# A new written order for a fused linear-attention and expert kernel: single products of zeros as units of the order, the first expert's w1 in two pieces, half of the last store on another queue

## The chip, the core and the metric

The kernel runs on one core of a Trainium2 chip. The core has five instruction streams that run beside each other: PE (TensorE, the matrix products; PEld are its weight loads), DVE (VectorE), ACT (ScalarE), POOL (GpSimd) and SP (SyncE, which here only issues DMAs). Each stream runs its instructions strictly in the order in which they were written, and waits on semaphores for the others. The metric is the device time of one execution in microseconds (us); lower is better.

## The reference

Linear attention over 8 batches, each of 8 heads, 576 positions and 64 features, followed by a mixture of 8 experts with a gate that may keep the expert of the position before:

```python
phi = lambda x: np.where(x > 0, x, np.exp(x) - 1.0) + 1.0
q_p, k_p = phi(q), phi(k)
kv  = einsum('bhsd,bhse->bhde', k_p, v);  z = k_p.sum(axis=2)
x   = einsum('bhsd,bhde->bhse', q_p, kv) / (einsum('bhsd,bhd->bhs', q_p, z)[..., None] + 1e-6)
x   = x.transpose(0, 2, 1, 3).reshape(B, S, 512)
logits = x @ w_gate                       # (B, S, 8)
local  = sigmoid(x @ w_local)             # below 0.5: take this position's own expert
for b in range(B):
    for s in range(S):
        fresh = argmax(logits[b, s])
        e = fresh if s == 0 or local[b, s] < 0.5 else prev
        prev = e
        out[b, s] = softmax(logits[b, s])[e] * (relu(x[b, s] @ w1[e]) @ w2[e])
```

## The kernel before

The kernel is written for the case that all positions of a batch keep the expert of its first position; a flag is computed on the way, and a general path behind it, which is not run here, handles everything else. So a batch needs one expert's weights, and they are known only when the logits of the batch's first position are there.

The work of one batch `b` is cut into named operations. Two of the eight heads lie in one 128-row tile, so a batch has two halves of four heads, numbered `n = 2b` and `n = 2b + 1`. For each half: loads `Lk`, `Lq`, `Lv` (SP); exponentials `E.k`, `E.q` (ACT), which give one part of phi; `E2` (the relu part) and `P` (the rest of phi); `VC` copies v next to a column of ones; `K` is the product k'v (PE, 64x64 tiles, f32), `KC` copies it out; `Q` transposes q (PE), `QC` copies it out; `N` is the numerator with the denominator in an extra column (PE, 64x64 tiles), `D` divides it (DVE) into x in bf16. `QL`, `QLC`, `NL`, `DL`, `XL`, `XLC` do the same for 64 of the 576 positions that are left over. Then, for the batch: `X` transposes x, `XC` copies it out; `R.b.0` computes the logits of the last chunk, which holds position 0, and `R.b.1` those of the other chunks, `RC` copies them out; `PK` picks the expert and looks it up in a small cache of three weight slots, `BK` keeps the cache's books; `W.b.0` and `W.b.1` (POOL) load w1 and w2 of the expert if it is not in the cache; `CW` copies them into the working tiles `w1cur` and `w2cur` (DVE); `S1`, `S2`, `S3` compute the gate's factor; `H.b.0` to `H.b.7` are x·w1 in eight chunks (PE, 128x128, bf16), `HC` their relu; `O0.b` and `O.b.0` to `O.b.4` are the product with w2, `OC` scales it out of PSUM into `yo` (or `yl` for the 64 left-over positions), `ST` stores it.

What runs when is written out by hand as one list of words, `ORDER` (lines 23 to 72). Every word is an operation; its instructions are added to the streams of their engines in the order of the list, and nothing is moved afterwards. A number behind a slash is the PSUM bank pair that the operation uses; an operation that uses a bank waits until the last user's result has been copied out. A `^` puts a copy on the other one of DVE and ACT than its default. Since each engine takes its own operations in the list's order, a word that stands earlier in the list also stands ahead of later ones on its engine, and whoever it waits for holds up what is behind it.

Three things in the list matter below. First, products of zeros: `fills` (line 111) is a table that puts so many `zero`·`zero` products of 128x512 on PE ahead of some operations; they compute nothing and keep PE at work while it would wait. Second, the first expert's weights: for batch 0 `weights` loads w1 straight into `w1cur`, in pieces whose columns are given by `FP` (line 224), and w2 into `w2cur`. `HOLD.0` and `HOLD.1` are two tiny DMAs on SP that read the last element of the first and of the second half of `w1cur`; they wait for that half to land, and so keep what is behind them on SP from being issued before. Third, the tiles `yo` and `yl` have two buffers each, so the result of batch b may be written only when the store of batch b - 2 has landed.

SP and ACT share eight completion semaphores for their DMAs, used in turn: a DMA that gets a semaphore waits until the last DMA on it has landed.

Of the kernel before, what the change touches and what calls it, by code (L numbers as in the profile page):

```python
# [23 lines left out]
Lq.0 Lk.1 FILL/0 Lv.1 Lv.1.1 Lv.0 Lk.0 Lq.1 Lv.0.1 E0.0 P0.0 E.k.1 CL.1 WT/1 E.q.0 P.k.1 QL.0/2 VC.1^  # L24
E2.q.0^ QLC.0 K.1/3 VC.1.1^ P.q.0.0 K.1.1 E.k.0 P.q.0 CL.0 Q.0/2 Lq.2 VC.0^ Lk.3 P.k.0 E.q.1 Lk.2 KC.1^
VC.0.1 QC.0 K.0/3 E2.q.1^ K.0.1 P.q.1.0 KC.0^ P.q.1 E.q.2 NL.0/2 N.0.0.1/3 DL.0 Lq.3 E.k.3 Lv.3 WG D.0.0.1
XL.0/2 Lv.2 Q.1/1 XLC.0^ R.0.0/2 QC.1 N.0.0.0/3 RC.0.0 D.0.0.0 W.0.0 E.k.2 N.0.1.1/2 N.0.1.0/1 PK.0 E2.k.3
D.0.1.1 E.q.3 D.0.1.0 BK.0 P.k.3 VC.3^ W.0.1 X.0.0/3 X.0.1/2 XC.0.0 XC.0.1^ K.3/1 E2.q.2^ E2.q.3^ R.0.1/3
HOLD.0 H.0.0/2 P.q.3 Lk.5 H.0.1/0 HC.0.0 P.q.2 H.0.2/2 HC.0.1 H.0.3/0 KC.3 RC.0.1 S1.0 QL.1/1 CW.0.0 Q.3/3
QLC.1 HC.0.2 H.0.4/1 E2.k.2 HC.0.3^ H.0.5/2 QC.3 P.k.2 Q.2/0 HC.0.4^ H.0.6/3 QC.2 VC.2 N.1.1.1/1 HC.0.5 Lv.5  # L30
K.2/0 Lq.4 S2.0 D.1.1.1 HC.0.6 Lv.4 Lk.4 N.1.1.0/2 KC.2 Lk.7 S3.0 NL.1/3 Lq.5 H.0.7/1 DL.1 O0.0/0 D.1.1.0
HC.0.7 E.k.5 XL.1/3 O.0.0 XLC.1^ N.1.0.1/1 E2.k.5^ OC.0.0 N.1.0.0/2 D.1.0.1 VC.5^ R.1.0/3 O.0.1/0 D.1.0.0
E.q.4 RC.1.0 PK.1 E2.q.4 X.1.0/1 O.0.2/2 OC.0.1 P.k.5 W.1.0 VC.4^ X.1.1/3 XC.1.0 O.0.3/0 Lv.7 XC.1.1^ P.q.4
E.k.4 R.1.1/1 Lq.6 K.5/3 OC.0.2 Lv.6 CW.1.0 E2.k.4 Lk.6 O.0.4/2 Lk.9 E.q.5 RC.1.1 P.k.4 H.1.0/1 KC.5^ OC.0.4
E2.q.5^ H.1.1/3 OC.0.3 P.q.5 HC.1.0 K.4/2 E.k.7 S1.1 Lq.7 H.1.2/0 E2.k.7 Lk.8 HC.1.1^ H.1.3/1 HC.1.2^ E.q.6
CW.0.1 QL.2/3 Q.4/0 QLC.2 HC.1.3 P.k.7 W.1.1 H.1.4/3 QC.4 H.1.5/1 E2.q.6^ HC.1.4 VC.7^ P.q.6 H.1.6/0 HC.1.5
Lv.10 K.7/3 KC.4 Lv.8 CW.1.1 HC.1.6 VC.6^ N.2.0.1/1 NL.2/2 KC.7 D.2.0.1 N.2.0.0/0 E.q.7 Lv.9 H.1.7/3 D.2.0.0
S2.1 Q.5/1 HC.1.7 E2.q.7^ E.k.6 O0.1/0 S3.1 QC.5 DL.2 O.1.0 O.1.1/3 P.q.7 OC.1.0 E2.k.6 BK.1 Lq.9 QL.3/2
E.k.8 XL.2/1 O.1.2/0 Lq.8 P.k.6 XLC.2^ QLC.3 E2.k.8^ OC.1.1 R.2.0/1 K.6/2 E.k.9 RC.2.0 PK.2 N.2.1.0/3 OC.1.2
Lk.10 N.2.1.1/1 KC.6 VC.8^ W.2.0 ST.0.0 D.2.1.0 NL.3/0 O.1.3/2 E.q.8 D.2.1.1 Lk.11 DL.3 W.2.1 Q.6/3 OC.1.3  # L40
P.k.8 XL.3/1 X.2.1/0 XLC.3^ X.2.0/2 QC.6 XC.2.1 O.1.4/1 CW.2.0 XC.2.0^ R.3.0/0 K.8/3 OC.1.4 E2.q.8^ E.q.9
N.3.0.1/2 RC.3.0 Lk.12 KC.8 P.q.8 R.2.1/1 ST.1.4 VC.9^ H.2.0/0 E2.q.9 VC.10 H.2.1/3 RC.2.1 D.3.0.1 Lv.13
HC.2.0 H.2.2/1 Lv.11 E2.k.9 Lq.10 BK.2 Q.7/0 ST.0.4 HC.2.1 P.k.9 H.2.3/2 QC.7 H.2.4/3 P.q.9 HC.2.2 HC.2.3
H.2.5/0 PK.3 E.k.10 Lq.11 H.2.6/1 HC.2.4^ W.3.0 K.9/2 S1.2 HC.2.5 CW.2.1 N.3.1.1/3 HC.2.6 Lk.13 N.3.1.0/0
S2.2 KC.9^ D.3.1.1 E.q.10 N.3.0.0/1 H.2.7/2 D.3.1.0 E.k.11 W.3.1 O0.2/3 HC.2.7^ E2.k.10 D.3.0.0 QL.4/0
X.3.1/2 QLC.4 S3.2 X.3.0/1 E2.k.11 O.2.0 Q.8/0 XC.3.1 E2.q.10 OC.2.0^ O.2.1/2 P.k.11 QC.8 XC.3.0 E.q.11
# [29 lines left out]
def kernel(  # L76
# [11 lines left out]
    nc = tc.nc  # L88
    P = 128
    B, H, S, Dh = q.shape  # L90
    D = H * Dh
    E = moe_w_gate.shape[1]
# [15 lines left out]
    NX = 3  # L108
    SLOTS = [2, 2, 2, 2]

    fills = {("WT",): 13, ("K", 1): 4, ("R", 0, 0): 5, ("X", 0, 0): 4, ("K", 3): 2}

    consts = ctx.enter_context(tc.tile_pool(name="consts", bufs=1))
    keep = ctx.enter_context(tc.tile_pool(name="keep", bufs=1))
# [876 lines left out]
```

## Time and profile before

| | us |
|---|---|
| three runs | 221.3, 221.81, 220.11; median 221.3 |
| the profiled execution: its own time | 219.5 |
| its span, first to last instruction | 217.7 |
| PE busy | 206.1 (95% of the span) |
| DVE busy | 177.8 (82%) |
| ACT busy | 131.3 (60%) |

All times inside the execution below are counted from the start of the span. The profiled execution took 219.5 us by the same clock as the runs, 1.8 us more than its span, and 1.8 us less than the median of the three runs. A row of the timeline gives start, duration, engine, line, operation, what is written and read, how many instructions were merged into the row, and in brackets the idle time ahead of it with what ended it. A row's duration ends with the last result, so the next row on the same engine may start up to 0.1 us earlier; where it matters, the time from one start to the next is used.

### The profile page before, as it was taken

The numbers are of one execution on the slowest core, as the hardware profiler recorded it, in microseconds if no ns is written. First come the engines' busy times: TensorE is split into PE (matmuls) and PEld (weight loads), VectorE is DVE, ScalarE is ACT, GpSimd is POOL, SyncE is SP. The second block draws the span as 40 slices with busy tenths as digits, with TensorE's granted clock in tenths as the row PEclk, the third lists the DMA queues.
The fourth block names the chain that finished last, engine by engine and source line by source line (L and its number), as shares of the span: only waits on it lengthen the run. The fifth ranks groups of instructions, "written<-read, shape, count | busy, mean of one in ns | idle before, by whom it ended". The sixth has DMA issues, their size and how long they took to land.

```text
span 217.7 us, 8573 instructions
## 1 busy us (share of the span) xinstructions
PE 206.1 (95%) x3704; PEld 150.5 (69%) x3719; DVE 177.8 (82%) x459; ACT 131.3 (60%) x197; POOL 13.6 (6%) x41
## 2 busy tenths in 40 slices
PE   7878799999999999999999999999999999999991
PEld 2466588657885798865889578875889578747640
DVE  0695988798999999998999989778897989586740
ACT  2687838699999999793358975483753302501110
POOL 4000500000200000300100000110000001100000
PEclk9889999999999999999999999999999999999999
DMA  5989999988975989999359878598320009999033
GB/s 190 369 248 380 215 183 237 334 318 306 360 266 175 308 322 285 343 210 203 66 189 307 311 274 287 104 181 145 123 99 3 5 15 370 177 162 268 5 132 121
DMA packets 24447, 46.77 MB, mean 215 GB/s; under 512 B 2124, under 2 KB 9808, under 8 KB 23508
## 3 DMA queue, kind: packets, MB, share of 16 engines
q1 hardware_dynamic: 16324, 37.49, 49.5%
q0 software_dynamic: 7392, 8.41, 24.7%
q8 instruction: 31, 0.51, 0.9%
q10 hardware_dynamic: 688, 0.26, 0.5%
q14 instruction: 12, 0.10, 0.1%
HBM read 61.88 MB, written 9.44 MB: 328 GB/s over the span
## 4 chain that ended last, share of the span: by engine, by line
PE 77%; DMA 11%; ACT 4%; DVE 3%; issue 2%; POOLq 0%; ACTq 0%; DVEq 0%
PE hps L556 26%; PE yps L578 22%; PE kvps L306 7%; PE nps L357 6%; DMA w1s<-in_moe_w_dram 5%; PE tq L317 5%; PE yps L582 3%; DMA kraw<-in_k_dram 3%; DMA kraw<-in_moe_w_gate_dram 3%; PE tx L391 3%; PE lps L433 1%; PE npl L376 1%; DVE xb L345 1%; PE fill L744 1%; PE tql L330 1%
## 5 line engine op out<-in xcount | busy, mean ns | idle before, releaser
L556 PE MATMUL hps<-xT,w1cur 128*128 128x288 bf16 x512 | 67.0, 286 | 0.0
L578 PE MATMUL yps<-w2cur,hT 128*128 128x512 bf16 x243 | 58.4, 379 | 0.7
L556 PEld LDWEIGHTS <-w1cur 128*128 128x128 bf16 x512 | 48.7, 98 | 12.9 <-issue 0.6
L565 ACT ACTIVATE hT<-hps 128x576 bf16<-128x576 f32 x41 | 26.8, 660 | 36.4 <-PE hps L556 27.4
L578 PEld LDWEIGHTS <-hT 128*128 128x128 bf16 x256 | 24.0, 98 | 25.5 <-issue 0.3
L345 DVE TENSOR_TENSOR xb<-nps,rec 128x512 bf16<-128x512 f32 x32 | 22.1, 692 | 1.1
L281 DVE SCALAR_TENSOR_TENSOR fq<-fq,qraw 128x576 f32<-128x576 f32 (+1 forms) x32 | 22.4, 744 | 0.2
L306 PE MATMUL kvps<-vone,kraw 64*64 64x65 f32 x1152 | 21.1, 225 | 1.0 <-ACT kv L292 0.8
L306 PEld LDWEIGHTS kvps<-vone,kraw 64*64 64x64 f32 x1152 | 19.2, 140 | 3.5 <-ACT vone L292 1.7
L241 ACT ACTIVATE ek<-kraw 128x1152 f32<-128x1152 f32 x16 | 18.8, 1172 | 3.4 <-DMA kraw<-in_k_dram 3.4
L567 DVE TENSOR_SCALAR hT<-hps 128x576 bf16<-128x576 f32 x23 | 17.1, 753 | 4.2 <-PE hps L556 4.0
L274 DVE SCALAR_TENSOR_TENSOR kraw<-ek,kraw 128x1152 f32<-128x1152 f32 x14 | 18.9, 1349 | 0.7 <-ACT kraw L248 0.7
L241 ACT ACTIVATE fq<-qraw 128x1152 f32<-128x1152 f32 (+1 forms) x16 | 18.5, 1157 | 1.3 <-DMA qraw<-in_q_dram 1.3
L357 PE MATMUL nps<-kv,qT 64*64 64x65 f32 x1024 | 19.0, 219 | 0.2
L593 ACT ACTIVATE yo<-yps,pr 128x512 f32<-128x512 f32 x16 | 11.1, 691 | 11.4 <-PE yps L578 11.3
L357 PEld LDWEIGHTS nps<-kv,qT 64*64 64x64 f32 x1024 | 16.8, 134 | 1.5 <-issue 0.5
L317 PE MATMUL tq<-ident,fq 128*128 128x128 f32 x128 | 16.7, 274 | 0.0
L292 ACT COPY qT<-tq 128x512 f32<-128x512 f32 x28 | 15.9, 641 | 0.6 <-PE tq L317 0.6
L292 ACT COPY xT<-tx 128x1024 bf16<-128x1024 bf16 x9 | 9.1, 1014 | 9.9 <-PE tx L391 9.7
L317 PEld LDWEIGHTS tq<-ident,fq 128*128 128x128 f32 x128 | 14.4, 141 | 0.7
L595 DVE TENSOR_SCALAR yo<-yps,pr 128x512 f32<-128x512 f32 x16 | 11.7, 745 | 2.0 <-PE yps L578 1.9
L248 ACT ACTIVATE kraw<-kraw 128x1152 f32<-128x1152 f32 x10 | 11.7, 1170 | 0.0
(106 smaller groups left out, 222.2 us busy)
## 6 DMA issues: line engine op xcount, KB each, us to landing
kraw<-in_k_dram SPq DMA_DIRECT2D x16, 576.0 KB, 7.3
qraw<-in_q_dram SPq DMA_DIRECT2D x14, 576.0 KB, 5.3
vraw<-in_v_dram SPq DMA_DIRECT2D x14, 576.0 KB, 5.7
w1s<-in_moe_w_dram POOLq DMA_DIRECT2D x7, 1024.0 KB, 10.4
w2s<-in_moe_w_dram POOLq DMA_DIRECT2D x7, 1024.0 KB, 13.1
out_dram<-yo SPq DMA_DIRECT2D x14, 512.0 KB, 4.6
qraw<-in_q_dram SPq DMA_DIRECT2D x2, 512.0 KB, 4.0
w2cur<-in_moe_w_dram POOLq DMA_DIRECT2D x1, 1024.0 KB
```

The lines of the kernel that those rows point to most:

```text
L241: nc.scalar.activation(e[:, :, c0:c1, :], raw_, Act.Exp)
L274: nc.vector.scalar_tensor_tensor(r, e, 1.0, r, Alu.min, Alu.add)
L281: nc.vector.scalar_tensor_tensor(e[:, g], e[:, g], 1.0, r[:, g], Alu.min, Alu.add)
L292: (nc.scalar.copy if on_act(*name, act=act) else nc.vector.tensor_copy)(dst, src)
L306: nc.tensor.matmul(ps[g * PH:(g + 1) * PH, t, :W], lhsT=f[h, g, c, :], rhs=vo[h, g, c, :], start=(c == 0), stop=(c == C - 1))
L317: nc.tensor.transpose(ps[:, r, i * P:(i + 1) * P], ex_[n, "q"][:, 1 + i + (NC - 1) * r, :, :], identity=ident)
L345: nc.vector.tensor_tensor(dst, ps[:, :, :, :Dh].rearrange("p g (i t) e -> p g i t e", t=2), rec.rearrange("p g (i t o) -> p g i t o", t=2, ...
L357: nc.tensor.matmul(ps[o * PH:(o + 1) * PH, g, (il * 2 + t) * W:(il * 2 + t + 1) * W], lhsT=qT[n][g * PH:(g + 1) * PH, t, i * P + o * PH:i ...
L556: nc.tensor.matmul(ps[:, u, :HS], lhsT=w1b[:, kk, m * P:(m + 1) * P], rhs=xT[b][:, kk, u * HS:(u + 1) * HS], start=(kk == 0), stop=(kk == ...
L565: nc.scalar.activation(dst, src, Act.Relu)
L567: nc.vector.tensor_scalar(dst, src, 0.0, None, Alu.max)
L578: nc.tensor.matmul(ps, lhsT=hT[b][:, m, i * P:(i + 1) * P], rhs=w2b[:, m, :], start=(m == 0), stop=(m == FK - 1))
```

## The change

Four things change:

1. `ORDER` is another list of the same operations. Banks, the engine of many copies, and the places of loads and stores differ. Relus and scalings that DVE did are fewer: 16 of the 64 `HC` instead of 23, and 14 of the 40 `OC` instead of 20; ACT does the rest.
2. The products of zeros: the table `fills` keeps only 16 ahead of `WT` (the transposes of the gate weights), where it had 28 in five places. 24 single products, `Z.0` to `Z.23`, are operations of their own in the list, all of them ahead of `H.0.0`: six ahead of `WT`, the others between `K.1` and `X.0.0`. Three small 32x32 products of zeros stand at the very start.
3. `FP` has two pieces instead of three, so that w1 of batch 0 comes in halves (columns 0 to 511, 512 to 1023) instead of a quarter, a quarter and a half. `HOLD.1` moves from the middle of the list to just behind `HOLD.0`.
4. Of the last store (`ST.7.4`, the 64 left-over positions of batch 7) only the first half is issued by ACT; the second half goes to SP.

```diff
-Lq.0 Lk.1 FILL/0 Lv.1 Lv.1.1 Lv.0 Lk.0 Lq.1 Lv.0.1 E0.0 P0.0 E.k.1 CL.1 WT/1 E.q.0 P.k.1 QL.0/2 VC.1^
...
+Lq.0 Lk.1 Z.21 Z.18 Lv.1 Z.11 Z.0 Z.13 Lv.1.1 Z.14 Lk.0 Lv.0 Lq.1 Lv.0.1 E0.0 P0.0 E.k.1 CL.1 E.q.0 P.k.1
...
-    fills = {("WT",): 13, ("K", 1): 4, ("R", 0, 0): 5, ("X", 0, 0): 4, ("K", 3): 2}
+    fills = {("WT",): 16}
...
-        FP = (0, F // 4, F // 2, F)
+        FP = (0, F // 2, F)
...
-                    eng = nc.scalar if b == B - 1 else nc.sync
+                    eng = nc.scalar if b == B - 1 and h == 0 else nc.sync
...
+        for i in range(24):
+            op(("Z", i), lambda: work(1))
...
+            for _ in range(3):
+                nc.tensor.matmul(fill[:32, :32], lhsT=zero[:, :32], rhs=zero[:, :32], start=True, stop=True)
             for name in order:
                 work(fills.get(name, 0))
```

The list itself tells little; the streams that come of it do. Three places follow, each before and after. Line numbers in these rows are one higher after the change than before for the same operation. The names end in the buffer's number: `kraw_71` and `qraw_73` hold k and q of half 3, `vraw_74` its v, `qraw_72` and `kraw_70` are of half 2.

The first place is ACT from the copy of the second `K` on, before the change. In turn: `KC.0`, `E.q.2`, `E.k.3`, `XLC.0`, `QC.1`, `E.k.2`, `E2.k.3`, `E.q.3`, `VC.3`, `XC.0.1`:

```order
L292 COPY kv<-kvps 128x130
L241 ACTIVATE fq<-qraw_72 128x2x9x64
L241 ACTIVATE ek<-kraw_71 128x1152
L292 COPY xT<-txl 128x2x2x64
L292 COPY qT<-tq 128x2x256 x2
L241 ACTIVATE ek<-kraw_70 128x1152
L248 ACTIVATE kraw_71<-kraw_71 128x1152
L241 ACTIVATE fq<-qraw_73 128x2x9x64
L292 COPY vone_78<-vraw_74 128x18x64
L292 COPY xT<-tx 128x4x256
```

The same stretch of ACT after the change: `KC.0`, `E.k.3`, `QC.1`, `E.q.2`, `E2.k.3`, `E.q.3`, `VC.3`, `E2.q.3`, `XC.0.0`, `E.k.2`:

```order
L293 COPY kv<-kvps 128x130
L242 ACTIVATE ek<-kraw_71 128x1152
L293 COPY qT<-tq 128x2x256 x2
L242 ACTIVATE fq<-qraw_72 128x2x9x64
L249 ACTIVATE kraw_71<-kraw_71 128x1152
L242 ACTIVATE fq<-qraw_73 128x2x9x64
L293 COPY vone_78<-vraw_74 128x18x64
L249 ACTIVATE qraw_73<-qraw_73 128x1152
L293 COPY xT<-tx 128x4x256
L242 ACTIVATE ek<-kraw_70 128x1152
```

`XLC.0` has left for DVE and `E.k.2` stands behind the copy of x now; `E.q.2` has moved from ahead of `E.k.3` to behind `QC.1`, and `E2.q.3`, the relu of `qraw_73`, which DVE did, stands ahead of the copy of x.

The second place is SP around the holds, before:

```order
L139 DMA qraw_73<-in_q_dram 128x2x576
L139 DMA vraw_74<-in_v_dram 128x2x576
L139 DMA vraw_76<-in_v_dram 128x2x576
L510 DMA there<-w1cur 1x1
L139 DMA kraw_69<-in_k_dram 128x2x576
L139 DMA vraw_76<-in_v_dram 128x2x576
```

And after (`kraw_69` is `Lk.5`, k of the second half of batch 2):

```order
L140 DMA qraw_73<-in_q_dram 128x2x576
L140 DMA vraw_74<-in_v_dram 128x2x576
L140 DMA vraw_76<-in_v_dram 128x2x576
L511 DMA there<-w1cur 1x1 x2
L140 DMA kraw_69<-in_k_dram 128x2x576
L140 DMA vraw_76<-in_v_dram 128x2x576
```

`Lk.5` now waits for both halves of w1, where it waited for the first.

The third place is SP around the store of batch 1, `ST.1.0`, before (`yo_1363` is batch 1's result; the tiles' names carry their buffer's number here):

```order
L139 DMA qraw0_72<-in_q_dram 128x2x576
L139 DMA qraw1_73<-in_q_dram 128x2x576
L139 DMA vraw0_74<-in_v_dram 128x2x576
L139 DMA kraw3_71<-in_k_dram 128x2x576
L602 DMA out_0_dram<-yo_1363 64x2048 x2
L139 DMA qraw0_72<-in_q_dram 128x2x576
```

And after (`yo_1385` and `yl_1386` are batch 1's):

```order
L140 DMA qraw0_72<-in_q_dram 128x2x576
L140 DMA vraw2_76<-in_v_dram 128x2x576
L140 DMA vraw0_74<-in_v_dram 128x2x576
L140 DMA kraw3_71<-in_k_dram 128x2x576
L608 DMA out_0_dram<-yl_1386 64x256 x2
L603 DMA out_0_dram<-yo_1385 64x2048 x2
L140 DMA kraw1_69<-in_k_dram 128x2x576
```

The two stores of `yl` have come in ahead of the two stores of `yo`, which batch 3's first result (`OC.3.0`, the same buffer) has to wait for. `OC.3.0` was done by DVE and is done by ACT now, and PE's `O.3.2` takes the bank that `O.3.0` used, where it took another one before.

## What was predicted

> **What bounds the kernel.** I began with the page: the span, and the engines' shares of it.
>
> ```profile
> span 217.7 us, 8573 instructions
> ...
> PE 206.1 (95%) x3704; PEld 150.5 (69%) x3719; DVE 177.8 (82%) x459; ACT 131.3 (60%) x197; POOL 13.6 (6%) x41
> ```
>
> PE is busy nearly throughout. Next I cut the span where the first expert product starts (`H.0.0`, 27.47) and where the last product ends (212.87). A row of this view gives the stretch, its length, then busy time and instructions of PE, PEld, DVE, ACT and POOL, the granted clock, the DMA share and GB/s. The fourth row is a window inside the start.
>
> ```profile
> 0.00:27.47 27.47, 21.60 (x456) 14.37 (x458) 18.10 (x42) 18.64 (x26) 5.59 (x20) 0.94 0.93 279
> 27.47:212.87 185.40, 184.54 (x3255) 136.10 (x3264) 159.24 (x417) 112.70 (x171) 8.03 (x21) 1.00 0.74 208
> 212.87:217.70 4.83, 0.00 (x0) 0.00 (x0) 0.48 (x1) 0.00 (x0) 0.00 (x0) 0.93 0.33 106
> ...
> 8.50:12.50 4.00, 4.00 (x79) 2.66 (x80) 3.80 (x5) 3.70 (x8) 0.00 (x0) 0.57 1.01 362
> ```
>
> Three stages follow. In the middle one, 185.4 us, PE idles 0.9 us in all and the work is the same before and after, so a new order can win next to nothing there; it can only lose, by a new wait or by dearer neighbours. The start is 27.5 us in which PE is partly fed with zeros, because it waits for what DVE, ACT and the loads prepare: above all there can an order win. The end is 4.8 us of last stores.
>
> So I read how `H.0.0` is reached, on PE first (timeline; the row at 31.77 is from the chain of waits, where overlaps are cut off).
>
> ```profile
> 27.05 0.56 PE L433 MATMUL lps<-wg,xT 128*128 128x9 bf16 x16
> 27.47 4.08 PE L556 MATMUL hps<-xT,w1cur 128*128 128x288 bf16 x32
> 31.39 0.38 PE L330 MATMUL tql<-ident,fq 128*128 128x128 f32 x2
> 31.77 0.87 PE tq L317 x8
> 35.31 1.14 PE L556 MATMUL hps<-xT,w1cur 128*128 128x288 bf16 x8
> 36.38 0.70 PE L357 MATMUL nps<-kv,qT 64*64 64x65 f32 x32
> ```
>
> `R.0.1` (27.05) is followed at once by four `H`, at (31.39 - 27.47)/4 = 0.98 us each; `Q.3` (0.87) comes behind them. After the change `Q.3` stands ahead of `H.0.0`. The comparison is therefore fair if `H.0.0` after starts at 27.47 + 0.87 = 28.34: later is a loss, earlier a gain.
>
> **The start, term by term.** `R.0.1` needs both copies `XC.0.0` and `XC.0.1`. After the change the first of them is at the end of ACT's stretch that the order shows. These are ACT's rows before.
>
> ```profile
> 18.35 1.16 ACT L241 ACTIVATE ek<-kraw 128x1152 f32<-128x1152 f32 x1 [1.31 <-DMA kraw<-in_k_dram]
> 19.42 0.35 ACT L292 COPY xT<-txl 128x256 bf16<-128x256 bf16 x1
> 19.67 1.13 ACT L292 COPY qT<-tq 128x512 f32<-128x512 f32 x2
> 20.67 1.18 ACT L241 ACTIVATE ek<-kraw 128x1152 f32<-128x1152 f32 x1
> 21.73 1.17 ACT L248 ACTIVATE kraw<-kraw 128x1152 f32<-128x1152 f32 x1
> 22.79 1.17 ACT L241 ACTIVATE fq<-qraw 128x1152 f32<-128x1152 f32 x1
> 24.07 1.16 ACT L292 COPY vone<-vraw 128x1152 f32<-128x1152 f32 x1
> 25.26 1.01 ACT L292 COPY xT<-tx 128x1024 bf16<-128x1024 bf16 x1
> ```
>
> ACT stood idle until 18.35 for k of half 3 (`E.k.3`). Before, `E.q.2` was already done in that idle time; after, it stands behind it. From start to start: `E.k.3` 1.07 (18.35 to 19.42), `QC.1` 1.00, a full-size exponential 1.06, a relu 1.06. After the change ACT therefore runs: `E.k.3` 18.35, `QC.1` 19.42, `E.q.2` 20.42, `E2.k.3` 21.48, `E.q.3` 22.54, and `VC.3` could start at 23.60. It needs v of half 3, for which the two rows below (the issue on SP, and the landing of that load) give 16.86 + 7.1 = 23.96.
>
> ```profile
> 16.86 0.92 SPq L139 DMA_DIRECT2D vraw<-in_v_dram  x2
> ...
> DMA to landing us min/median/max: 7.1/7.1/7.1
> ```
>
> So `VC.3` at 24.0, `E2.q.3` at 25.1, `XC.0.0` at 26.2, done at 27.2; `R.0.1` 0.42, `Q.3` 0.87, and `H.0.0` at 28.5 to 28.6, against 28.34. I take +0.25 us. The lower end is the case that ACT does not end last (rival A, -0.8). For the upper end every operation counts with its full duration instead of start to start: 1.16, 1.13, 1.17 three times, 1.16, 1.17 and 1.01 from 18.35 on end at 27.5, and 0.56 and 0.87 behind them make 28.9: +0.6.
>
> The halves of w1 cost nothing in this sum. Rows of POOL's issue, the landing of the two quarters, the first hold on SP, the copy that waits for the second half, and the load behind the hold with its landing:
>
> ```profile
> 21.89 2.31 POOL L499 DMA_DIRECT2D w1cur<-in_moe_w_dram  x3 [18.13 <-DVE rec L344]
> DMA to landing us min/median/max: 5.0/5.4/5.7
> 28.41 0.75 SPq L510 DMA_DIRECT2D there<-w1cur  x1
> 29.20 0.37 SPq L139 DMA_DIRECT2D kraw<-in_k_dram  x1
> DMA to landing us min/median/max: 7.8/7.8/7.8
> 31.98 1.23 DVE L514 COPY w1s<-w1cur 128x4096 bf16<-128x4096 bf16 x1 [0.66 <-DMA w1cur<-in_moe_w_dram]
> ```
>
> The second quarter had landed by 28.41, so a first half that lands no later than that is there when `H.0.0` wants it at 28.5; at worst 0.1. POOL issues two pieces instead of three, some 0.77 sooner for w2 (2.31/3), which nobody waits for at that point. The zeros: 43 products instead of 28, all ahead of `H.0.0`, where PE waits anyway; cover is the idle time that the old ones filled, and if a row of them outlasts its wait, one costs about 0.22 (estimate from the `H` rows: 0.98/8 for 288 columns, so 0.22 for 512). The idle stretch ahead of `R.0.1` remains open for this, so zero.
>
> **The middle.** Two terms. First, PE's neighbours: eight products of `H` take 0.98 behind each other, but 35.31 to 36.38 = 1.07 where 64x64 products follow. Every such change of tile shape costs about 0.1. Counted in the two orders from `H.0.0` on, there are 50 such changes before and 52 after: +0.2, between 0 and 0.3. Over the whole list it is 60 against 71, since the zeros (128x128) stand between 64x64 groups.
>
> The Trainium skill, TensorEngine Tiling (Array Packing), section Key Properties, says that changing the tiling mode drains TensorE. The trace agrees, with 0.1 us each, and that rule speaks against this change: if all eleven added changes lay on the path, the term would be +1.1 instead of +0.2. Nine of them lie ahead of `H.0.0`, in PE's waiting time.
>
> Second, a new wait: `OC.3.0` needs the buffer that `ST.1.0` stores, and PE's `O.3.2` needs the bank that `OC.3.0` empties. Rows of that store before, with the landing of its first half; of a pair of `yl` stores; of PE at `O.3.1` and `O.3.2`; and ACT's group of such scalings (691 ns each):
>
> ```profile
> 113.50 1.14 SPq L602 DMA_DIRECT2D out_dram<-yo  x2
> DMA to landing us min/median/max: 7.6/7.6/7.6
> 120.07 1.98 SPq L607 DMA_DIRECT2D out_dram<-yl  x2
> 122.41 3.63 PE L578 MATMUL yps<-w2cur,hT 128*128 128x512 bf16 x16
> L593 ACT ACTIVATE yo<-yps,pr 128x512 f32<-128x512 f32 x16 | 11.1, 691 | 11.4 <-PE yps L578 11.3
> ```
>
> With two `yl` stores ahead (1.5 to 2.0 us of issue) the second `yo` store goes out at 115.6 to 116.1 rather than 114.1 and lands 7.6 us later, 123.2 to 123.7; as the second of the pair it may land up to 1.1 later (the pair's issue took 1.14): 123.2 to 124.8. `OC.3.0` takes 0.7, so the bank is free at 123.9 to 125.5. PE wants it at 122.41 + 3.63/2 + the moves above, about 124.6. The wait is 0 to 0.9; I take +0.35, the store's own row being the nearest and pointing to the lower half. The relus and scalings that go from DVE to ACT (13) cost nothing: ACT is 60% busy, and DVE, at 82%, is relieved.
>
> **The end.** Rows of SP's last two stores of `yo`, of ACT's two stores of `yl`, and SP's last long wait:
>
> ```profile
> 212.60 1.11 SPq L602 DMA_DIRECT2D out_dram<-yo  x2
> 213.40 1.68 ACTq L607 DMA_DIRECT2D out_dram<-yl  x2
> ...
> SPq L986 <- DMA out_dram<-yo: 2.1, 1, 2.1
> ```
>
> The second half of `yl` is issued at about 214.0 by ACT; SP is free at 213.7 and can issue it 0.3 earlier, but what SP's final wait ended on was a `yo` store. I take -0.15; between -0.45 (all of the gain and a shorter list on ACT) and +0.3 (the `yl` half queues behind `yo`).
>
> **Sum.** +0.25 + 0.35 + 0.2 - 0.15 = +0.65. The profiled execution would go from 219.5 to 220.15. The runs' median stands 1.8 above that execution; I carry the difference over: 221.3 + 0.65 = 222.0.
>
> **Rivals.** A: ACT is not what ends last. `XLC.0` no longer queues behind `E.k.3`; on DVE it can follow the division that the first row shows, at 18.5, and be done at 18.9 instead of 19.77. All of DVE moves up 0.87:
>
> ```profile
> 17.84 0.69 DVE L345 TENSOR_TENSOR xb<-nps,rec 128x512 bf16<-128x512 f32 x1
> 26.10 1.42 DVE L252 TENSOR_SCALAR qraw<-qraw 128x1152 f32<-128x1152 f32 x2
> 27.56 2.77 DVE L281 SCALAR_TENSOR_TENSOR fq<-fq,qraw 128x576 f32<-128x576 f32 x4
> ```
>
> Before, DVE had its copy of x done at 26.10, where the second row starts; now at 25.2. `P.q.3` (2.77/2 = 1.39, the third row holds it and `P.q.2`) ends at 26.6, `Q.3` at 27.5, and there `H.0.0` starts: 0.84 below 28.34, and 1.1 below my term, 220.9. For it: DVE is the bound of the start before. Against it: ACT's chain above, whose start at 18.35 is a load.
>
> B: the clock. In 8.5 to 12.5 us the granted clock was 0.57 with PE busy throughout. The profiled execution is 1.8 faster than the median, which could mean that other runs pay one more such window where it hurts, and that zeros prevent it. One window of 3.4 us at half clock costs at most 1.7: 222.0 - 1.7 = 220.3. The Trainium skill, TensorE: Matmul & The Clock Gate, section What's actually happening, has a free-running window of 3.4 us, by which the place of the half clock would differ from run to run; one trace cannot show that.
>
> C, on the other side: the second hold. `Lk.5` left at 29.20 behind the first; after, it leaves when the second half has landed, by the copy's row as late as 32.0, and lands 7.8 later, 39.8. ACT has `E.k.5` and `E2.k.5` (2.1) ahead of `HC.0.7` (0.7 at most), which `O.0.0` needs. Before, `O0.0` started at
>
> ```profile
> 40.02 1.67 PE L578 MATMUL yps<-w2cur,hT 128*128 128x512 bf16 x6
> ```
>
> so with its seven products `O.0.0` is due at 40.02 + 7 x 0.22 + 0.25 = 41.8. From a landing of 39.0 on PE waits: at 39.8 it is 0.8, and each us by which w1 lands later adds one; with 1 to 2 of them, since w2 shares its queue, 223.8 to 224.8. For it: 7.8 us for one load is the longest of these. Against: the expert is known up to 0.87 earlier, and SP's load has the queue to itself.
>
> D: nothing of this reaches the path: 221.3.
>
> **How the numbers follow.** The forecast 0.45, A 0.13, B 0.12, C 0.15, D 0.15. Within 1% of 221.3, which is about what a measurement of this kernel can tell from no change, means 219.1 to 223.5. Faster by more takes A and B together (219.2) and the end's gain: 0.16 with what I have overlooked. Slower: C's 0.15 and the upper ends of the forecast's terms (+0.6 + 0.9 + 0.3 + 0.3 = 2.1, 223.4): 0.18. The rest, 0.66, is the same. The range runs from A and B together to C's lower price: 219.2 to 224.0.
>
> **What would show it.** In the profile after: `E.k.3` idle ahead of it until about 18.4, then ACT without a gap to `XC.0.0` at 26 to 27, and `H.0.0` at 28.5; if `H.0.0` starts at 27.5, A is right. PE's waits would list `yps` on an ACT scaling near 125, of 0 to 0.9 us; a wait of `yps` near 42 on a relu is C. A granted clock of 1.00 in 8.5 to 12.5 shows that the zeros work; three runs close to the profiled one show B. PE's end should be 0.8 later than 212.87. A middle stage with PE idle over 2 us would prove the sum wrong.

## The result and the profile after

| | us |
|---|---|
| four runs after the change | 228.82, 226.1, 226.4, 227.39; median 226.9 |
| four runs before, on the same chip | 221.3, 221.81, 220.11, 220.09; median 220.7 |
| ratio after to before | 1.029, 95% interval 1.020 to 1.037 |
| the profiled execution after | 228.8 (span 227.2), the slowest of the four |
| the profiled execution before | 219.5 (span 217.7) |

The change makes the kernel slower by 5.7 to 6.2 us, depending on which of the runs before it is compared with. The forecast was 222.0 and its range ended at 224.0. Ratios here and below leave out disturbed executions, so they need not be the quotient of two medians; of the four runs of e4 and of e5 two remain each, and of the profiles of e4 and e11, which are disturbed, only the end of e4 is read.

First the page of the kernel after, its span and the engines' shares:

```profile
span 227.2 us, 8615 instructions
...
PE 212.2 (93%) x3734; PEld 152.3 (67%) x3734; DVE 170.0 (75%) x448; ACT 139.5 (61%) x208; POOL 13.3 (6%) x40
```

The span has grown by 9.5, PE's busy time by 6.1. About 2.9 of that are products of zeros (12.0 after, 9.1 before), all of it in the start, where they fill time in which PE waits; the half clock shown below adds 1.7. The stretches cut as in the prediction, at `H.0.0` and at PE's last product, then four short windows of the same view (length, then busy time and instructions of PE, PEld, DVE, ACT and POOL, granted clock, DMA share, GB/s):

```profile
0.00:30.49 30.49, 25.73 (x481) 17.12 (x481) 20.33 (x48) 19.22 (x26) 4.85 (x19) 0.94 0.94 273
30.49:220.58 190.09, 186.51 (x3256) 135.15 (x3253) 149.13 (x400) 120.31 (x182) 8.49 (x21) 0.99 0.69 199
220.58:227.19 6.61, 0.00 (x1) 0.00 (x0) 0.48 (x1) 0.00 (x0) 0.00 (x0) 0.67 0.33 108
127.34:130.26 2.92, 0.00 (x0) 0.00 (x0) 2.29 (x3) 0.74 (x2) 0.00 (x0) 1.00 1.00 323
130.26:134.50 4.24, 4.24 (x12) 1.56 (x12) 0.00 (x0) 3.63 (x5) 0.00 (x0) 0.60 0.74 302
11.00:14.60 3.60, 3.60 (x43) 2.88 (x44) 3.50 (x6) 2.98 (x5) 0.00 (x0) 0.53 0.78 241
```

All three stages lose. `H.0.0` starts at 30.49, which is 2.15 later than the fair reference of 28.34. The middle, 190.09, stands against 185.37 - 0.87 = 184.50 (`Q.3` has left it): 5.6 more. The end is 6.61 instead of 4.83: 1.8 more. Inside the middle PE does nothing for 2.92 us, and right behind that it works 4.24 us at a granted clock of 0.60. The clock's records have 0.5 from 130.61 to 134.02; that costs 3.41/2 = 1.7. Next, for whom PE waited (us in total, times, the longest):

```profile
PE yps L579 <- ACT yo L594: 2.9, 1, 2.9
PE nps L358 <- issue: 1.7, 2, 1.1
...
PE kvps L307 <- ACT vone L293: 0.9, 1, 0.9
PE tq L318 <- issue: 0.8, 1, 0.8
```

The first row is the new wait of the prediction, eight times its size. For the rows with "issue" the same view of before has only this one:

```profile
PE fill L744 <- issue: 0.2, 1, 0.2
```

After the change PE waits for nothing that the profile shows, in the middle of an operation, three times. These idle times are taken up below.

So the 9.5 us of the profiled execution go to: start 2.15, a third "issue" idle time at 44.90 0.61, the wait at 130 2.92, the half clock behind it 1.7, what is left of the middle 0.4 (5.6 less these three), the end 1.8. The sum is 9.6, for 9.5. The other three runs are 1.4 to 2.7 shorter than this one; two of them have a mean granted clock of 0.99 instead of 0.975. So the split holds for the profiled execution; how much each of these terms took in the other runs is not known.

**The store.** SP's rows around `ST.1.0`, then the pieces of the chain of waits (start, us, what) from its second store to PE:

```profile
115.11 0.37 SPq L140 DMA_DIRECT2D qraw<-in_q_dram  x1
115.53 1.76 SPq L140 DMA_DIRECT2D vraw<-in_v_dram  x2
117.34 0.47 SPq L140 DMA_DIRECT2D kraw<-in_k_dram  x1
117.85 1.96 SPq L608 DMA_DIRECT2D out_dram<-yl  x2
119.86 1.27 SPq L603 DMA_DIRECT2D out_dram<-yo  x2
```

```profile
120.51 8.91 DMA out_dram<-yo
...
129.52 0.70 ACT yo L594
130.22 0.04 issue
130.26 5.30 PE yps L579 x16
```

PE reached `O.3.2` at 127.34, which is the predicted 124.6 plus the 2.7 by which everything was late by then. The store was not: predicted were an issue at 115.6 to 116.1 and a landing 7.6 to 8.7 later; measured were 120.51 and 8.91.

**The end.** SP's rows behind PE's last products, and ACT's one:

```profile
218.11 1.24 SPq L608 DMA_DIRECT2D out_dram<-yl  x2
219.45 3.73 SPq L603 DMA_DIRECT2D out_dram<-yo  x4
221.14 0.58 ACTq L608 DMA_DIRECT2D out_dram<-yl  x1
223.28 0.54 SPq L608 DMA_DIRECT2D out_dram<-yl  x1
```

ACT is free at 221.72. SP, to which the second half was moved, comes to it only at 223.28, since the last of its four `yo` stores takes from 221.32 to 223.18.

**The idle times called "issue".** PE's rows at the first two of them:

```profile
22.05 0.50 PE L358 MATMUL nps<-kv,qT 64*64 64x65 f32 x17
23.63 0.46 PE L358 MATMUL nps<-kv,qT 64*64 64x65 f32 x15 [1.08 <-issue]
...
28.62 0.41 PE L318 MATMUL tq<-ident,fq 128*128 128x128 f32 x2
29.84 0.81 PE L318 MATMUL tq<-ident,fq 128*128 128x128 f32 x6 [0.81 <-issue]
```

One operation is cut in two. By the trace's count of PE's instructions (weight loads, products and a few of its sequencer) the three idle times begin behind the 705th, the 960th and the 1473rd: 255 and 513 apart. The page's list of DMA queues has one for instructions:

```profile
q8 instruction: 31, 0.51, 0.9%
```

These packets bring PE's own program: 29 of the 31 fall into PE's working time, one for every 259 of its 7512 recorded instructions (7512/29), and each has 16 KB (0.51 MB/31). In the trace the second, third and fifth of them land at 22.31, 28.40 and 43.47; PE goes on at 23.63, 29.84 and 44.90, 1.3 to 1.4 later each time. If a border lies at every 256th instruction, counted so that 705 is one, then 26 of the 28 packets of before that can be set against a border landed about 2 us or more before PE came to it, the other two 1.5 and 1.7; after, the three named ones landed 0.02, 0.36 and 0.60 before, and all others at least 1.5. In these two traces that separates the stalls from the borders without one.

The Trainium skill, Runtime: NRT & Kernel Launch, section Instruction fetch mechanics, has instructions streamed in 16 KiB blocks of 256, with the cost of a border mostly hidden. The block agrees with 255 and 513. That it is hidden holds for the trace before (0.16 us) and not for this one (2.5 us).

### The profile page after: what moved, and what is told of

It is laid out like the page before. It is cut to its first block, busy times and chain, and to the rows that moved or that the text cites. A ratio compares the mean times of both kernels' runs of the same rounds, so it can differ in the third digit from the quotient of the medians.

```text
span 227.2 us, 8615 instructions
## 1 busy us (share of the span) xinstructions
PE 212.2 (93%) x3734; PEld 152.3 (67%) x3734; DVE 170.0 (75%) x448; ACT 139.5 (61%) x208; POOL 13.3 (6%) x40
## 4 chain that ended last, share of the span: by engine, by line
PE 77%; DMA 11%; SPq 3%; ACT 3%; DVE 2%; issue 2%; ACTq 0%
PE hps L557 26%; PE yps L579 22%; PE kvps L307 8%; PE tq L318 6%; PE nps L358 6%; DMA out_dram<-yo 4%; DMA vraw<-in_v_dram 3%; PE yps L583 3%; DMA kraw<-in_k_dram 3%; PE tx L392 2%; PE lps L434 1%; SPq L140 1%; SPq L608 1%; ACT qraw L249 1%; DMA out_dram<-yl 1%
## 5 line engine op out<-in xcount | busy, mean ns | idle before, releaser
L579 PE MATMUL yps<-w2cur,hT 128*128 128x512 bf16 x256 | 60.7, 387 | 2.9 <-ACT yo L594 2.9
L557 PEld LDWEIGHTS <-w1cur 128*128 128x128 bf16 x512 | 48.9, 98 | 12.5 <-DVE pr L550 0.2
L566 ACT ACTIVATE hT<-hps 128x576 bf16<-128x576 f32 x48 | 30.8, 653 | 27.3 <-PE hps L557 27.3
L594 ACT ACTIVATE yo<-yps,pr 128x512 f32<-128x512 f32 x21 | 14.3, 689 | 20.8 <-PE yps L579 16.3
L318 PE MATMUL tq<-ident,fq 128*128 128x128 f32 x128 | 17.7, 284 | 0.9 <-issue 0.8
L596 DVE TENSOR_SCALAR yo<-yps,pr 128x512 f32<-128x512 f32 x11 | 8.2, 746 | 12.2 <-PE yps L579 12.2
L293 ACT COPY qT<-tq 128x512 f32<-128x512 f32 x26 | 14.8, 631 | 0.3
L568 DVE TENSOR_SCALAR hT<-hps 128x576 bf16<-128x576 f32 x16 | 11.9, 751 | 3.8 <-PE hps L557 3.8
L293 ACT COPY vone<-vraw 128x1152 f32<-128x1152 f32 (+2 forms) x13 | 13.6, 1049 | 0.5 <-DMA vraw<-in_v_dram 0.5
L747 PE MATMUL fill<-zero 128*128 128x512 bf16 x40 | 11.7, 427 | 0.0
```

What stands on the lines that cost most here:

```text
L293: (nc.scalar.copy if on_act(*name, act=act) else nc.vector.tensor_copy)(dst, src)
L318: nc.tensor.transpose(ps[:, r, i * P:(i + 1) * P], ex_[n, "q"][:, 1 + i + (NC - 1) * r, :, :], identity=ident)
L557: nc.tensor.matmul(ps[:, u, :HS], lhsT=w1b[:, kk, m * P:(m + 1) * P], rhs=xT[b][:, kk, u * HS:(u + 1) * HS], start=(kk == 0), stop=(kk == ...
L566: nc.scalar.activation(dst, src, Act.Relu)
L579: nc.tensor.matmul(ps, lhsT=hT[b][:, m, i * P:(i + 1) * P], rhs=w2b[:, m, :], start=(m == 0), stop=(m == FK - 1))
L594: nc.scalar.activation(dst, src, Act.Copy, scale=pr[:, i:i + 1])
```

## The experiments

Each kernel is compared with the kernel before, run on the same chip beside it (medians 221.1, 221.4 and 221.1 for the three groups of four). "Middle" is the time from `H.0.0` to PE's last product.

**e1: the store of batch 1 earlier.** In the list, `ST.1.0` goes ahead of `Lq.12`:

```diff
-E2.k.12^ Lq.12 H.3.5/0 ... D.4.0.0 ST.1.0 N.4.1.0/2
+E2.k.12^ ST.1.0 Lq.12 H.3.5/0 ... D.4.0.0 N.4.1.0/2
```

> The changed kernel with one word moved: ST.1.0, the two stores of yo of batch 1, stands ahead of the load of q (half 12) that SP holds back until 115.11 in the trace of after, instead of behind the two stores of yl. Theory 1 (the late store is the cause of PE's wait of 2.92 us at 130.26 and, through that idle time, of the half clock in the 3.4 us behind it): the store lands near 119, PE's yps wait is gone, the granted clock stays 1.00 around 130. Time about 226.9 - 2.9 = 224.0, and a profile that had the half-clock stretch gains 1.7 more. Rival (the time is only moved: the loads behind the store go out 1.2 us later and PE waits for one of them, or for the next store): 226 to 227, with a new wait of 2 us or more on PE between 120 and 145.

Measured: 225.5, ratio 1.020 (1.011 to 1.029), against 1.029. The stores went out at 111.74 and 112.28 and had landed by 120.74; PE's wait is gone, and the clock is full where it was halved. The window 115 to 135 of e1:

```profile
115.00:135.00 20.00, 19.52 (x426) 14.18 (x424) 16.11 (x47) 13.16 (x21) 0.55 (x3) 1.00 0.80 302
```

Of the 0.48 that PE lacks there, 0.38 is one "issue" idle time, in `K` at 120.31. The wait did not come back elsewhere, so theory 1 holds for the wait and for the clock. Profile against profile the middle is 3.8 shorter (186.32 against 190.09), and `H.0.0` comes at 30.96 instead of 30.49, with idle times of 0.81 and 1.63 called "issue" ahead of it. The median fell by 1.4 only, not by 2.9 or more. The profiled execution of after was its slowest; what its other runs paid for the wait is not on record, so this difference stays open.

**e2: `ST.1.0` and `ST.1.4` exchanged.**

```diff
-ST.1.4 H.3.7/0 HC.3.6 D.4.0.0 ST.1.0
+ST.1.0 H.3.7/0 HC.3.6 D.4.0.0 ST.1.4
```

> The changed kernel with ST.1.0 and ST.1.4 exchanged, so that the yo stores of batch 1 stand ahead of the yl stores as before the change; nothing else. Theory 1a (the issue of the two yl stores, 117.85 to 119.82 in the trace of after, is what makes the yo store late, as the prediction's term had it): the second yo store goes out 2.0 us sooner, at 118.5, lands at 127.4, OC.3.0 ends at 128.2, PE's wait is 0.9 instead of 2.9; time about 224.9. Rival (the landing is set by the queue of data, 8.9 us here against 7.6 before, and by SP's earlier wait until 115.11, not by those two issues): landing stays at 128.5 to 129.4, PE waits 2.0 to 2.9, time 226 to 227.

Measured: 226.25, ratio 1.025 (1.016 to 1.033). The second `yo` store went out at 117.17, 1.9 sooner than after (1.5 of the 3.3 is because everything was 1.5 earlier there). It took about 9.8 us to land instead of 8.9 (reckoned back from PE's start, 0.85 as in the chain of after), and PE still waited:

```profile
PE yps L579 <- ACT yo L594: 1.9, 1, 1.9
```

So half of the gain in issue was lost in landing: the two `yl` stores ahead are worth 1.0 of the 2.9, not 2.0. The rest is that the store stands behind four loads of 576 KB, of which the first waits for DVE; both theories had a part. The clock stayed at 1.00 behind this wait of 1.95.

**e3: the borders of the instruction packets moved.** 64 small products more and 8 large ones less, at the very start, where PE waits for the gate weights anyway:

```diff
-    fills = {("WT",): 16}
+    fills = {("WT",): 8}
...
-            for _ in range(3):
+            for _ in range(67):
```

> The changed kernel with 67 small 32x32 products of zeros at the very start instead of 3, and 8 instead of 16 products of 128x512 zeros ahead of WT: PE's stream grows by 112 instructions ahead of everything else, in time in which PE waits for the gate weights anyway (they land at 7.82). Theory 2 (PE's idle times that the profile calls issue, 1.08 at 23.63, 0.81 at 29.84, 0.61 at 44.90, are PE's own instructions arriving late: each ends 1.3 to 1.4 us after a 16 KB packet of the instruction queue has landed, at 22.31, 28.40 and 43.47; where such a packet falls in the stream is decided by the count of instructions ahead of it): the three idle times leave these products and turn up elsewhere or not at all; H.0.0 starts 0.8 to 1.9 us sooner than 30.49, time 224.5 to 226 if no new ones take their place. Rival (they come of the loads that fill the DMA queues at these times, wherever the packets fall): idle times of the same size at the same products, time 226 to 227.5.

Measured: 239.2, ratio 1.085 (1.075 to 1.096), 12 us slower than the changed kernel. The three idle times did move, but the new place is far worse than the old one. PE's waits in e3:

```profile
PE nps L358 <- issue: 5.4, 5, 1.5
PE yps L579 <- issue: 3.3, 2, 3.1
PE npl L377 <- ACT fq L242: 2.3, 1, 2.3
...
PE tq L318 <- issue: 1.2, 1, 1.2
```

What was expected of the time is missed by 13 us or more; that the place of the borders matters is what it shows, and e5 tells it from the number of products. 112 instructions further on, borders fall at both ends of runs of `N` and `K`: four of the times from border to border are about 2 us in this trace, where the shortest of after is 4.6. The row `npl` ends at a border too: the packet landed at 125.76, PE went on at 126.71, and the profile names ACT.

**e4: the last store as before the change.**

```diff
-                    eng = nc.scalar if b == B - 1 and h == 0 else nc.sync
+                    eng = nc.scalar if b == B - 1 else nc.sync
```

> The changed kernel with both halves of the last yl store on ACT, as before the change. Theory 3 (SP is the later queue: its last yo store is issued from 221.32 to 223.18 and the yl half goes out at 223.28, while ACT would be free at 221.72): the end after PE's last product shrinks from 6.6 to about 5.2 us, time about 225.5. Rival (the prediction's term: SP is no later than ACT, the half on SP gains 0.15): 226.9 to 227.1, with the end as long as before or longer.

Measured: 1.022 (1.012 to 1.032); that can't be told from after's 1.029 (225.05 and 226.72 in the two runs that remain). The end can: 5.55 us behind PE's last product, where after, e1 and e2 have 6.61, 6.53 and 6.55. The later kernels agree: 8.2 in e3 and 6.20 in e5, which store as after, and 5.3 to 5.8 in e8, e9, e10 and e12, which store as e4. SP is the later queue; theory 3 has the direction and about the size (it said 5.2).

**e5: the borders moved by one whole block.** 147 small products instead of 3 and no large ones ahead of `WT`, together 256 instructions.

```diff
-    fills = {("WT",): 16}
+    fills = {}
...
-            for _ in range(3):
+            for _ in range(147):
```

> The changed kernel with 147 small products of zeros at the very start instead of 3, and none of the 16 large ones ahead of WT: PE's stream grows by 256 instructions. The idle times called issue in the profile of after begin 255 and 513 instructions of PE apart, so a 16 KB packet is taken to hold 256 instructions, and with 256 more ahead every later packet border falls at the same product as after the change, while e3 with 112 more was 12 us slower. Theory 2 (the place of the borders decides): within 2 us of the changed kernel, 225 to 229, issue idle times only where after, e1 and e4 have them (first 50 us). Rival (the many small products, or the lost large ones, cost the 12 us, by the clock or by the length of the stream): 237 or more.

Measured: 226.77 and 229.02 in the two runs that remain, against 225 to 229 expected. From two runs that can't be told from the changed kernel (226.1 to 228.82); it is at least 8.5 less than the fastest run of e3, which has 80 small products fewer. PE's rows for "issue" are one, 0.8 us at 46.11, in the same `N` as in after. So it is the place of the borders that cost e3 its 12 us, not the number of small products. In the start of e5, unlike that of after, PE waited 3.4 for copies of v and worked at half clock from 29.07 to 32.49.

**e6: the kernel before, with its borders moved.**

```diff
-    fills = {("WT",): 13, ("K", 1): 4, ("R", 0, 0): 5, ("X", 0, 0): 4, ("K", 3): 2}
+    fills = {("WT",): 5, ("K", 1): 4, ("R", 0, 0): 5, ("X", 0, 0): 4, ("K", 3): 2}
...
+            for _ in range(64):
+                nc.tensor.matmul(fill[:32, :32], lhsT=zero[:, :32], rhs=zero[:, :32], start=True, stop=True)
```

> The kernel before with 64 small products of zeros at the very start and 5 instead of 13 large ones there: 112 instructions more ahead of everything, no other change. Theory 2: the kernel before is only fast with its own packet borders. Taking the times between borders from its trace, moved by 112 instructions, four intervals of 256 instructions would last 2.3 us or less, against 3.6 at the shortest as it is; summed over all intervals, what lacks to 4.2 us (about what a packet needs from one border until its instructions run, estimated from the three idle times of after) is 11.8 against 1.1. So 229 to 233, with issue idle times in N and K between 35 and 180 us. Rival (the new written order alone brings the idle times): 220 to 222.5.

Measured: 235.9, ratio 1.071 (1.063 to 1.079), 14.5 us above the kernel before with the same written order. PE's waits:

```profile
PE nps L357 <- issue: 3.5, 3, 1.6
PE yps L578 <- DVE xb L345: 2.2, 1, 2.2
PE lps L433 <- issue: 2.1, 1, 2.1
...
PE hps L556 <- issue: 1.7, 2, 1.4
```

More than the 229 to 233 expected: the idle times in the middle sum to 9.8, near the 11.8 reckoned, but two of them (2.11 at 127.5 and 2.24 at 161.8) were each followed by 3.4 us at half clock, which the reckoning left out. The second is the row put down to DVE; it counts among them since PE went on 1.54 after a packet had landed (160.26), with a border there.

**e7: the kernel before with w1 in halves.**

```diff
-        FP = (0, F // 4, F // 2, F)
+        FP = (0, F // 2, F)
```

> The kernel before with w1 of batch 0 in halves (FP in two pieces), HOLD.1 and all else as before. Theory 4 (a half is later than a quarter: in the trace of after the first half landed at 29.66, 7.7 us after its issue, in e2 PE waited 0.32 at 28.93 for it; the first quarter before had landed by 27.47): H.0.0 starts between 28.4 and 29.7 instead of 27.47 and waits for w1cur, H.0.1 and all behind follow; 1 to 2 us more, 222 to 223. Rival (the prediction's term, at most 0.1): H.0.0 by 27.6, 221 to 221.3.

Measured: 224.73, ratio 1.019 (1.014 to 1.024), 3.4 more. The first half landed 8.1 us after its issue, at 29.88, 1.5 later than both quarters together had been there before (28.39). PE's longest wait, and the window behind it:

```profile
PE hps L556 <- DMA w1cur<-in_moe_w_dram: 2.4, 1, 2.4
```

```profile
27.51:29.93 2.42, 0.01 (x2) 0.01 (x1) 2.42 (x4) 0.00 (x0) 0.00 (x0) 1.00 1.10 163
29.93:34.00 4.07, 4.07 (x20) 2.71 (x21) 2.25 (x7) 1.10 (x2) 0.00 (x0) 0.58 1.23 205
```

`H.0.0` at 29.93 instead of 27.47, and the 2.42 us of idle PE are again followed by half clock (30.43 to 33.84), 1.7 more. Theory 4 holds, and the price is above its range because of the clock.

**e8: three repairs in the changed kernel.** e1 and e4 together, and `ST.6.4` ahead of `ST.7.0`:

```diff
-ST.7.0 O.7.3/1 OC.7.2 ST.6.4 ST.7.2
+ST.6.4 ST.7.0 O.7.3/1 OC.7.2 ST.7.2
```

> The changed kernel with three repairs: ST.1.0 early (as in e1), both halves of the last store on ACT (as in e4), and ST.6.4 ahead of ST.7.0 on SP, as before the change. Theory 1 and 3 together: no yps wait near 130, no half clock there, the end behind PE's last product 4.8 to 5.1 us instead of 6.5; what is left above before is the start with its issue idle times (0.5 to 3 us), 0.35 for w1 and 0.6 in the middle: 222.5 to 224.5. Rival (the wait and the tail were not what cost the time, and the rest grows): 225 or more.

Measured: 222.85, ratio 1.006 (1.002 to 1.010): 4.0 less than the changed kernel, and 1.5 above the median before. PE's waits in e8 from the second row on (the first, at the very start, is as before):

```profile
PE kvps L307 <- ACT vone L293: 1.2, 3, 0.6
PE kvps L307 <- issue: 1.0, 1, 1.0
PE nps L358 <- issue: 0.7, 1, 0.7
PE nps L358 <- ACT qT L293: 0.7, 1, 0.7
PE lps L434 <- ACT xT L293: 0.7, 1, 0.7
```

`H.0.0` starts at 28.79, the end is 5.77. Part of the 4.0 is that the start of this profile, unlike that of after, has no "issue" idle time, though PE's stream and its borders there are the same. The traces of e2, e9, e10 and e12 have none there either (beside 0.16 in a product of zeros), that of e1 has 0.81 and 1.63: whether the first two borders stall differs from trace to trace, and the reason is not shown. The third, in `N` between 42 and 46, cost 0.4 to 0.8 in after, e1, e5, e8, e9, e10 and e12, and 0.16 in e2. The row of 1.0 in `K`, at 118.68, is a new one: in e1, e8, e9, e10 and e12, which have the store early, PE stalls 0.38 to 1.59 there, and not in after, e2 and e5. The end is no shorter than e4's, so the place of `ST.6.4` did nothing that shows.

**e9: e8 with w1 in three pieces again** (`FP` as before the change, `HOLD.1` left behind `HOLD.0`).

```diff
-        FP = (0, F // 2, F)
+        FP = (0, F // 4, F // 2, F)
```

> e8 with w1 of batch 0 in a quarter, a quarter and a half again, as before the change; HOLD.1 stays behind HOLD.0. Theory 4 (the half lands 7.7 to 8.1 us after the issue of w1, the two quarters had both landed 6.5 after it): the wait for w1 no longer bounds H.0.0, which then follows ACT's chain: R.0.1 at 27.2 to 27.9, H.0.0 at 28.3 to 28.8, where e8 has 28.79. So in this order the halves cost 0 to 0.5: 222.3 to 222.9. Rival (the halves cost here what they cost in the kernel before, 3.3): 219.5 to 220.

Measured: 223.01, ratio 1.008 (1.004 to 1.012): the same as e8. In the order after the change the halves cost nothing that can be measured in the time, where in the order before they cost 3.4. In e9 the first quarter landed at 28.5 and `H.0.0` started at 29.52: other work of the start ends as late. (This profile has half clock from 21.98 to 25.40.) The halves are not free of waits: in e8 the half landed at 28.74, just as `H.0.0` began, and in e2 and e12 PE waited 0.32 and 0.65 for it.

**e10: e9 with `E.q.2` ahead of `E.k.3` on ACT.**

```diff
-DL.0 Lq.3 E.k.3 Q.1/0 ... RC.0.0 E.q.2 Z.16
+DL.0 Lq.3 E.q.2 E.k.3 Q.1/0 ... RC.0.0 Z.16
```

> e9 with one exponential moved: E.q.2 (q of half 2) ahead of E.k.3 on ACT, as before the change, where ACT stands idle until k of half 3 lands near 18.4. Theory (the prediction's first term: behind E.k.3 every operation of ACT's chain up to XC.0.0 comes 1.06 later): XC.0.0 is done 1.0 earlier, R.0.1 starts near 26.3 to 26.6 if DVE is as early, H.0.0 at 27.5 to 27.9; 1.0 less than e9, 221.3 to 221.9. Rival (DVE's phi of half 3 and the products K.3 or the instruction packets bound the start as well): H.0.0 no earlier than 28.3, same time as e9.

Measured: 224.79, ratio 1.014 (1.005 to 1.023), no gain. The rival holds for this profile, as ACT's rows show:

```profile
20.73 1.17 ACT L249 ACTIVATE kraw<-kraw 128x1152 f32<-128x1152 f32 x1
23.17 1.16 ACT L242 ACTIVATE fq<-qraw 128x1152 f32<-128x1152 f32 x1 [1.27 <-DVE rec L345]
24.63 1.15 ACT L293 COPY vone<-vraw 128x1152 f32<-128x1152 f32 x1 [0.30 <-DMA vraw<-in_v_dram]
```

The time that ACT gains it waits again, ahead of `E.q.3`; q of half 3 landed at 23.09, and v of half 3 at 24.55. The loads set ACT's chain from there on, not the exponential's place; q came 0.5 to 0.6 later than in e8 and e9 (22.49 and 22.60), so what the move would give with an earlier load is not shown. `H.0.0` came at 29.36, and two "issue" idle times in the middle, 1.59 and 0.60, add to the time.

**e11: the kernel before with 16 instead of 13 products of zeros ahead of `WT`.**

```diff
-    fills = {("WT",): 13, ("K", 1): 4, ("R", 0, 0): 5, ("X", 0, 0): 4, ("K", 3): 2}
+    fills = {("WT",): 16, ("K", 1): 4, ("R", 0, 0): 5, ("X", 0, 0): 4, ("K", 3): 2}
```

> The kernel before with 16 instead of 13 products of zeros ahead of WT: the change's zeros at that place alone. PE's stream grows by 6 instructions, which moves no packet border into a run of K or N. Prediction's rival B (zeros take away a half-clock stretch, worth up to 1.7): the granted clock is 1.00 from 5 to 217 and the time 219.6 to 220.5. Theory (the start waits for DVE, ACT and loads, not for PE's clock): same as before, 221.0 to 221.7, whatever the clock does near 10.

Measured: 223.96, ratio 1.011 (1.003 to 1.020), runs from 221.54 to 227.99. Rival B's gain is not there. Whether it is slower by itself stays open.

**e12: one load more in a quiet stretch.** The weights of batch 6 are loaded although they are in the cache:

```diff
-                    in_=src, cond=wl[b][2] > 0)
+                    in_=src, **({} if b == 6 else dict(cond=wl[b][2] > 0)))
```

> e8 with the condition of batch 6's weight loads taken away: the 2 MB of w1 and w2 of its expert are loaded once more into the cache slot that already holds them, in the stretch from about 169 to 181 in which nearly nothing is loaded otherwise. Theory 2a (instruction packets come late because they share the DMA engines with loads): the packets of the borders that PE passes in that stretch start 2 to 6 us after the border, where e8 had them between 1.6 ahead and 1.2 behind, and PE may show an issue idle time behind 170. Rival (their delay has nothing to do with the loads, but with where the products stand): they start as in e8, within 0.5 us.

Measured: one run, 224.7. Between 170 and 180 the DMA share rose from 0.01 to about 1.05. One packet of PE's queue fell into that stretch: it started 1.25 us behind its border, where in e8 it had started 1.54 ahead of it. It was later by 2.8, but not by as much as the 2 to 6 behind the border that were expected, and it is one packet. That loads delay the packets is supported by this, not settled. In the traces of before and after, packets in stretches without loads start at most 1.0 us behind their border; those that start more than 2 behind it (up to 6.0) all lie where loads keep the DMA engines busy.

## Why the prediction was wrong

**The step that failed** is the second term of the middle, "The wait is 0 to 0.9; I take +0.35", with the sentence "A middle stage with PE idle over 2 us would prove the sum wrong" that came true. The mechanism was right (`OC.3.0` waits for the landing of `ST.1.0`, PE for the bank), and so was the time at which PE wants the bank. The size was not: 2.92, and 2.3 in e5. The term was worked out from the row of the store before, moved by the two `yl` issues alone. Measured against before, once the general delay of 2.7 is taken off, the load at the head of that group was 1.1 later (it waits for DVE), two issues on SP took 1.25 and 1.44 where one had before, and the data took 1.3 more than 7.6 to land. The rows before gave no warning of the first; for the second they showed one slow issue (1.45 us, in the pair of `yl`), and the range had room for the landing alone. And nothing in the sum stood for the clock: the idle time halves PE's speed for 3.4 us behind it, 1.7 more, so in the profiled execution the wait of 2.9 cost 4.6.

**A cause that the sum did not have** is PE's own instructions. The trace before showed it with 0.16 us only, and the prediction has no term for it. It cost the profiled execution 1.08, 0.81 and 0.61; e3 and e6 show that a shift of 112 instructions with an unchanged order costs 12 and 14.5 us. The change adds 30 instructions ahead of `H.0.0` and then deals all operations anew, so every border lies elsewhere. By the trace of after, its shortest time between borders is 4.6 us, against about 3.5 before: by that measure the middle is no worse off than before, though a border in `K` stalls once the store is early (e8). In the profiled execution it is in and just behind the start, full of loads, that three packets came too late. Since e2 and e8, with the same stream, do not stall in the start, the new order alone does not explain it: the packets' arrival differs between executions.

**The start**, +0.25, otherwise: ACT went as forecast. `E.k.3` started at 18.53 (18.35 predicted), `VC.3` at 24.35 (24.0), the copy of x ended at 27.46 (27.2). In e8, which lost nothing to "issue" there, `H.0.0` came at 28.79 instead of 28.5 to 28.6. So the term was right within 0.3. Its second thought, that `E.q.2`'s new place is what costs, finds no support in e10.

**The halves of w1**, "0, at worst 0.1": wrong. The half landed at 29.66, not by 28.41; had PE been there on time it would have waited for more than 1 us. It did not show because `Q.3` was itself held until 29.84, and e9 shows that the order after the change does not feel it. Alone, in the order before, it costs 3.4 (e7). The failing thought was that a piece of the same bytes lands when the two smaller ones had.

**The zeros**, 0: right, as far as e11 tells; rival B's 1.7 did not come. After has a half-clock stretch in 11 to 14.6, and before had one in 8.5 to 12.5; e2 and e8, with the zeros of after, have none there, so the zeros do not decide whether it comes.

**Changes of tile shape**, +0.2: the middle without its idle times and without half clock is 184.9 to 185.2 in e1, e2 and e8, against 184.5 before, so 0.4 to 0.7. The sign is right, the rest of it is not explained.

**The end**, -0.15: wrong in sign. The store on SP makes it longer by about 1 us (e4: 5.55 against 6.5). The prediction had looked at when SP was free before, and not at the two stores of `yl` (`ST.6.4`) that the new order had put between the last `yo` stores; but with `ST.6.4` moved back and ACT storing both halves the end is still 5.77 in e8, against 4.83. Part of the remaining 0.9 is that the two `yl` stores took 3.6 us to land in e8 (median), 3.1 before; why stays open.

**The rivals.** A and B did not occur. C did not either: `Lk.5` left at 32.88 and landed at 39.83, as its worst case had it, yet `HC.0.7` did not hold up `O.0.0`; e2 alone shows 0.36 there. D is excluded by all of it. The chance of 0.18 for slower by over 1% was too low since two terms that were bounded one by one, the wait and the end, both came out beyond their upper ends, and the half clock behind the wait added a second price to it. The range, too, was said to end at C's lower price, which the working gives as 223.8, not 224.0; that changes nothing here.

## What to carry to other kernels

Before a new order is judged by its waits, look for idle times in the middle of an operation that are put down to nothing, count the instructions between them, and shift the stream by a few dozen dummies: if the time jumps by some per cent, a comparison of two orders is in part one of where instruction packets begin. A wait of over two microseconds on TensorE should be priced with and without half a clock window on top (1.7 here): six of seven such idle times had one. And a store that frees a buffer has to be priced from where its queue stands after the change, behind every load that waits for another engine, not from its own row before.

## What was not expected of the hardware

- PE's program comes in packets of 16 KB. In dense runs of 64x64 products PE takes 256 instructions in about 1.9 us (near the shortest time between borders in e3), less than the 1 us that a packet takes plus the 1.3 to 1.4 until it is used. With a border at each end of such a run PE stalled even without loads (idle 1.38 at 96.4 in e3, where the packet started 0.8 behind its border).
- Issues of DMAs on SP and ACT are often slow while such a packet moves: in the traces of before and after, of those that overlap a packet of an instruction queue 19 of 44 took over 0.7 us (up to 2.15), of the others 15 of 134. The store issue of 1.86 us at the end of after is one of them.
- Idle PE and clock: 2.92, 2.34, 2.42, 2.11, 2.24 and 3.09 us of idle PE (after, e5, e7, twice e6, e3) were followed or overlapped by 3.41 us at half clock; 1.95 (e2) and 2.29 (e3 at 126.7) were not. Half clock also came with shorter ones: 1.47 and 0.47 in e9 (from 21.98), 0.86 and 0.69 in e5 (from 29.07); 1.46 in e5, at 14, had none. The Trainium skill, TensorE: Matmul & The Clock Gate, section What's actually happening, has a free-running window of 3413 ns, after an idle one of which the clock is halved. The 3.41 agree; idle times shorter than a whole window were enough here.
